# Windowed attention and two MLPs on one core: tiles 6 to 8 turned by VectorE and DRAM, their scores moved into the second chunk

## The chip, the cores and the metric

The kernel runs on one core of one Trainium2 chip. The metric is the device time of a run in microseconds (us); lower is better. Outputs are fp32.

## The reference

```python
scores = (1 / np.sqrt(64)) * np.matmul(q, k.transpose(0, 1, 3, 2))     # 4 x 8 x 576 x 64
rel = pos[:, None] - pos[None, :]
scores = np.where((rel >= 0) & (rel < 64), scores, -1e9)
attn = np.exp(scores - scores.max(-1, keepdims=True))
attn = attn / (attn.sum(-1, keepdims=True) + 1e-9)
x = np.matmul(attn, v).transpose(0, 2, 1, 3).reshape(2304, 512)
...
h = x @ w_in                       # 512 -> 2048, first MLP
x = np.maximum(0.01 * h, h) @ w_out
...
h = x @ w_in2                      # 512 -> 2048, second MLP
out = (np.maximum(h, 0) + np.log1p(np.exp(-np.abs(h)))) @ w_out2
```

## The kernel before, in words

The 2304 tokens are 18 tiles of 128 tokens. Three tiles make a chunk of 384 tokens, so there are six chunks. A tile goes through attention: scores of a 64-wide window on TensorE (`tile_bp`, tile names `ps`), mask and maximum on VectorE (`att_bm` L503, `att_bn` L509), exponentials on ScalarE (`att_be` L520), one over the sums on VectorE (`att_bs`), the product with it on GpSimd (`att_bx` L533), probabilities turned so that keys lie on partitions (into `pair`), and probabilities times values on TensorE (`tile_dp` L909, name `po`). A chunk then goes through the first MLP: for each of 16 steps j a block of 12 matmuls makes 128 hidden columns (`gemm1_p`, name `ph`), ScalarE applies the activation (`gemm1_a` L630, name `g`) and rounds it (`gemm1_h`, `gh`), VectorE takes the rest (`gemm1_l` L642, `gl`), and a second block of 12 matmuls adds it to the output (`gemm2`, name `o`). Every fp32 product is made of three products of rounded high and low parts (`three`, L610 to L612).

The first chunk's steps 0 to 7, then the whole second chunk, are written out by hand in the string `HEAD`, one token for each piece of work, and `ordered` ties each engine's instructions to that order. Tokens are a letter and a number. `G`, `P`, `Q`, `R`, `H` are the five pieces of an MLP step (`gemm1_p`, `gemm1_a`, `gemm1_h`, `gemm1_l`, `gemm2`); numbers 0 to 7 are the first chunk's steps, 8 to 23 the second chunk's, so `P17` makes the tile `g_1_9`. `l`, `a`, `b`, `c`, `d` load one 512 KB weight piece (`wraw`, from `load_w` L147 or L152, three buffers) and convert it: `a` on ScalarE (L161), `b` on VectorE (L166, L168), `c` the high part, `d` the low part on VectorE (L246). `l18`/`l19` are step 9's pieces `wraw_9_0`/`wraw_9_1`, `l20` is `wraw_10_0`, `l24` is `wraw_12_0`. `Lq`, `Lv` load queries and keys, and values; `Bx`, `Cp`, `Ca`, `Dp` are pieces of attention by group (two groups to a tile: 10 and 11 are tile 5), `Cp` is four TensorE transposes (`att_cp` L542, name `pt`) and `Ca` ScalarE's copy of them into `pair`.

After `HEAD` a loop runs the first chunk's steps 8 to 15, then chunks 2 to 5. It has two slots for each step; the table `SLOTS` says in which slot each tile of the next chunk begins its scores and in which its `po` comes, and `attention_slots` hangs the other pieces on these. Tiles 6 to 8 (chunk 2) are prepared in the first chunk's steps 8 to 15, tiles from 9 on during chunks 2 to 5.

From tile `BY_DVE` = 6 on, queries and keys are not transposed by TensorE. `lay_out` (L405) re-lays them through DRAM, from `q`, `k` into `qd`, `kd`, by DMAs of 128-byte runs that SP issues; each is called a relay below. `load_blocks` (L414) brings a tile's part back, and VectorE transposes 32x32 blocks (`tile_u` L889, L890). From tile 9 on the probabilities go a like way: `turn` (L924) transposes blocks on VectorE into `pair`, `cross` writes `pair` to DRAM, `back` reads it in four DMAs. Tiles 6 to 8 have their probabilities turned by TensorE (`att_cp`) and copied by ScalarE (`att_ca`).

The relays of the second and third batch element (`relay`) are not tied to the order: the scheduler puts them among the weight loads on SP, the one engine that issues these DMAs.

Of the kernel before, what the change touches and what calls it, by code (L numbers as in the profile page):

```python
# [8 lines left out]
F32 = mybir.dt.float32  # L9
# [12 lines left out]
def tile_window_attention_two_mlps(  # L22
# [387 lines left out]
    def load_blocks(t):  # L410
        for n, (src, nm) in enumerate(((qd, "q"), (kd, "k"))):
            a = kept[("part", "cv")[n]][:, 2 * DM :] if t >= THIRDS else kept["64"][t % 2].bitcast(F32)[:, n * DM : (n + 1) * DM]
            a = a.rearrange("p (n x) -> p n x", n=NP)
            nc.sync.dma_start(a, src[:, :, t * P : (t + 1) * P])  # L414
            qk_raw[nm, t] = a
# [501 lines left out]
    in_blocks = lambda h: pair[:, h].rearrange("r p x -> r (p x)").rearrange("r (a p c) -> r p a c", p=NP, c=TB)  # L917

    def turn(g):


        t, h = g
        sm = st.pop(g)
        nc.vector.transpose(in_blocks(h), sm.rearrange("r p (b c) -> r p b c", c=TB))  # L924
        st[g] = in_blocks(h)

    def cross(t):

# [14 lines left out]
    def attention_slots(c, n_slots):  # L943

        at = {}
        late = n_slots > 16
        put = lambda n, *todo: at.setdefault(n if late else max(n, -3), []).extend(todo)
        for n in range(TPC):
            t = c * TPC + n
            s, d = SLOTS.get(c, LATER)[n]  # L950
            two = ((t, 0), (t, 1))
            put(s - 6, (att_ah, (t,)))
            put(s - 3, (tile_u, (t,)))
            put(s - 2, (att_aq, (t, "")))
# [17 lines left out]
    SLOTS = {2: ((0, 6), (5, 11), (10, 15)), 3: ((1, 12), (10, 21), (19, 30))}  # L972
# [24 lines left out]
        d14 G7 Be10 a11 Q5 d13 P6 Bs10 Q6 a16 R6 Bx11 Bx10 P7 Cp10 b11 Lv5 b16 Cp11 l15 Ca11 H6 Ca10 c11  # L997
        Dp5 a18 d11 Q7 R5 c16 H5 Dh5 l17 a15 b18 Dl5 G8 d16 b15 c18v a17 P8 c15v R7 d15 G16 P16 G11 P11
# [5 lines left out]
        R18 P9 P21 d23 G22 Q9 R9 H9 c31v Q21 R21 d31 G23 H20 P22 Q19 P23 H21 H18 Q23 R19 Q22 H19 R23 R22  # L1004
# [44 lines left out]
    relay = {CUT + NF - AHEAD - 2 + n: (lay_out, first, range(n * PARTS // 2, (n + 1) * PARTS // 2)) for n in range(2)}  # L1049
    relay |= {CUT + NF - AHEAD + n: (lay_out, first + 1, range(n * PARTS // 4, (n + 1) * PARTS // 4)) for n in range(4)}  # L1050
    begun = 0

    for item in HEAD:
        name = item.rstrip("vg")
        kind = name.rstrip("0123456789")
        n = int(name[len(kind) :])

        held.pop(next((ps for ps, f in READ.items() if f == kind), "") + f"_{n}", None)
        if kind == "G":
            if not begun:  # L1060
                att_tags[:] = ["att"]
            if begun in relay:
                f, *a = relay[begun]
                f(*a)
            if begun == CUT + NF - AHEAD:
                keep_places()
                load_qk(BY_DVE)
                load_qk(BY_DVE + 1)
                load_v(BY_DVE)
            begun += 1  # L1070
        if kind in pieces_by:
            ordered(queues, pieces_by[kind], n, item[len(name) :])
        else:
            ordered(queues, pieces[kind], n)

# [25 lines left out]
    at_slot = {}  # L1101
    base = {}
    slot = 0
    for n, (c, j, s, e, nxt) in enumerate(steps):
        if n < CUT + NF:
            continue
        if s and nxt is not None:
            left = next(i for i in range(n, len(steps)) if steps[i][3]) - n + 1
            base[c] = 2 * (n - CUT - NF), 2 * left, nxt
    for first_slot, n_slots, nxt in base.values():  # L1110
        for i, todo in attention_slots(nxt, n_slots).items():
            at_slot.setdefault(first_slot + i, []).extend(todo)
    for i in sorted(at_slot):
        if i < 0:
            for f, a in at_slot[i]:
                ordered(queues, f, *a)

    for n, (c, j, s, e, nxt) in enumerate(steps):
# [6 lines left out]
        strict = True  # L1125
        run = (lambda f, *a: ordered(queues, f, *a)) if strict else (lambda f, *a: f(*a))
        for u in range(2):
            todo = at_slot.get(2 * (n - CUT - NF) + u, ())
            on_pe = (tile_bp, att_cp)
            run(save_x2)  # L1130
            for f, a in todo:
                if f in on_pe:
                    run(f, *a)
                elif f is tile_d:
                    run(tile_dp, a[0], ((a[0], 0), (a[0], 1)))
            if u == 0:
                run(gemm1_p, c, j)
            elif strict:
                run(gemm1_a, c, j)
                run(gemm1_h, c, j)  # L1140
            for f, a in todo:
                if f is tile_d:
                    x = x_of(a[0] // TPC)
                    run(att_dh, a[0], "", x[0])
                    run(att_dl, a[0], *x)
                elif f not in on_pe:
                    run(f, *a)
            if u == 1 and strict:
                run(gemm1_l, c, j)
            for _ in range(ticks(c, j, u)):  # L1150
                if strict:
                    run(next, keeper, None)
                else:
                    later(next, keeper, None, lag=1)
# [139 lines left out]
```

## Time and profile before

| what | value |
|---|---|
| runs | 838.16, 838.77, 841.83 us; median 838.77 |
| the profiled run's own time | 839.48 us |
| its span, first to last instruction | 837.7 us |
| TensorE busy | 819.9 us, 98% of the span |
| VectorE, ScalarE, GpSimd busy | 616.2, 431.8, 209.0 us |
| DMA | 157.99 MB, mean 189 GB/s |
| granted TensorE clock, mean over the span | 1.000 of full speed |

The profiled run's own time is its span and what lies around it, 1.8 us here. The profile's chain is the work that ended last, followed back from the last instruction: what lies on it sets the time.

### The profile page before, as it was taken

How to read it: one execution, taken by the hardware profiler on the slowest of the kernel's cores; microseconds unless marked ns; L12 is line 12 of the kernel's file. 1: busy time of each engine (PE TensorE's matmuls, PEld its weight loads, DVE VectorE, ACT ScalarE, POOL GpSimd, SP SyncE). 2: the span in 40 equal slices, each digit the busy share in tenths (PEclk: the TensorE clock that was granted, in tenths of full speed). 3: DMA queues.
4: the chain of work that ended last, by engine and by line, in shares of the span. 5: the costliest groups of instructions: out<-in, count | busy, mean ns of one | idle time of the engine just before them, and what ended most of it. 6: DMA issues, size and time to landing. Idle time of an engine off the chain costs nothing.

```text
span 837.7 us, 16547 instructions
## 1 busy us (share of the span) xinstructions
PE 819.9 (98%) x6096; PEld 803.4 (96%) x6096; DVE 616.2 (74%) x1152; ACT 431.8 (52%) x981; POOL 209.0 (25%) x262
## 2 busy tenths in 40 slices
PE   5899999999999999999999999999999999999997
PEld 4799999999999999999999999999999999999997
DVE  5987763446555655554458799998889998989896
ACT  6966533544444454444466655656544454445342
POOL 3211000213333332233125415555511700000000
PEclk9999999999999999999999999999999999999999
DMA  9977667646998979978595544535568884343423
GB/s 224 245 208 201 179 160 140 173 91 188 229 243 253 261 194 253 274 215 219 184 262 170 183 152 148 177 128 169 178 211 264 258 301 151 101 152 101 139 66 100
DMA packets 225505, 157.99 MB, mean 189 GB/s; under 512 B 105488, under 2 KB 194704, under 8 KB 225424
## 3 DMA queue, kind: packets, MB, share of 16 engines
q1 hardware_dynamic: 225424, 156.93, 65.6%
q8 instruction: 48, 0.79, 0.4%
q14 instruction: 33, 0.27, 0.1%
HBM read 103.94 MB, written 59.24 MB: 195 GB/s over the span
## 4 chain that ended last, share of the span: by engine, by line
PE 95%; DVE 2%; DMA 1%; ACT 1%; issue 1%; POOL 0%; SPq 0%; DVEq 0%; ACTq 0%; POOLq 0%
PE ph L610 8%; PE o L610 8%; PE ph L611 8%; PE ph L612 8%; PE o L612 8%; PE o L611 8%; PE f L854 7%; PE f L846 7%; PE f L853 7%; PE p L612 7%; PE p L611 7%; PE p L610 7%; PE po L909 2%; PE ps L485 2%; PE pt L542 1%
## 5 line engine op out<-in xcount | busy, mean ns | idle before, releaser
L610 PE MATMUL ph<-xh,w 128*128 128x384 f32 x384 | 130.5, 340 | 0.0
L610 PE MATMUL o<-gh,w 128*128 128x384 f32 x384 | 130.1, 339 | 0.0
L612 PE MATMUL ph<-xh,w 128*128 128x384 f32 x384 | 128.6, 335 | 0.0
L611 PE MATMUL ph<-xl,w 128*128 128x384 f32 x384 | 128.6, 335 | 0.0
L611 PE MATMUL o<-gl,w 128*128 128x384 f32 x384 | 128.5, 335 | 0.0
L642 DVE TENSOR_TENSOR gl<-g,gh 128x384 fp32r<-128x384 f32 x96 | 57.2, 595 | 90.6 <-ACT gh L636 88.9
L630 ACT ACTIVATE g<-ph 128x384 f32<-128x384 f32 x96 | 46.7, 489 | 145.6 <-PE ph L612 138.2
L612 PE MATMUL o<-gh,w 128*128 128x384 f32 x360 | 120.5, 335 | 0.0
L533 POOL TENSOR_TENSOR sm<-sm,sums 128x512 f32<-128x512 f32 x36 | 39.4, 1095 | 146.4 <-DVE sums L529 135.5
L610 PEld LDWEIGHTS ph<-xh,w 128*128 128x128 f32 x384 | 72.1, 188 | 1.9 <-issue 1.2
L610 PEld LDWEIGHTS o<-gh,w 128*128 128x128 f32 x384 | 72.1, 188 | 1.6 <-issue 1.0
L611 PEld LDWEIGHTS ph<-xl,w 128*128 128x128 f32 x384 | 72.2, 188 | 0.2 <-DVE xl L560 0.2
L612 PEld LDWEIGHTS ph<-xh,w 128*128 128x128 f32 x384 | 72.1, 188 | 0.2 <-DVE w L246 0.2
L611 PEld LDWEIGHTS o<-gl,w 128*128 128x128 f32 x384 | 72.1, 188 | 0.0
L854 PE MATMUL f<-wq,a 128*128 128x256 f32 x252 | 71.5, 284 | 0.0
L853 PE MATMUL f<-wq,a 128*128 128x256 f32 x252 | 71.4, 283 | 0.0
L846 PE MATMUL f<-wq,a 128*128 128x256 f32 x252 | 71.4, 283 | 0.0
L612 PEld LDWEIGHTS o<-gh,w 128*128 128x128 f32 x360 | 67.6, 188 | 0.0
L520 ACT ACTIVATE sm<-sm,nm 128x128 f32<-128x128 f32 x144 | 55.9, 392 | 7.5 <-DVE nm L509 7.5
L636 ACT CAST gh<-g 128x384 fp32r<-128x384 f32 x96 | 49.2, 513 | 15.2 <-PE o L612 11.5
L854 PEld LDWEIGHTS f<-wq,a 128*128 128x128 f32 x252 | 48.4, 192 | 0.2 <-DVE a L803 0.2
L853 PEld LDWEIGHTS f<-wq,a 128*128 128x128 f32 x252 | 48.4, 192 | 0.0
(310 smaller groups left out, 2185.5 us busy)
## 6 DMA issues: line engine op xcount, KB each, us to landing
in<-hd SPq DMA_DIRECT2D x32, 512.0 KB, 4.8
wraw<-in_moe_w_in_dram SPq DMA_DIRECT2D x16, 512.0 KB, 4.0
wraw<-in_moe_w_out_dram SPq DMA_DIRECT2D x16, 512.0 KB, 4.4
kept<-in_moe_w_in_dram SPq DMA_DIRECT2D x16, 512.0 KB, 5.8
kept<-in_moe_w_out_dram SPq DMA_DIRECT2D x16, 512.0 KB, 4.4
hd<-kept SPq DMA_DIRECT2D x19, 384.0 KB, 2.6
hd<-cv SPq DMA_DIRECT2D x15, 384.0 KB, 2.6
wd<-cv SPq DMA_DIRECT2D x11, 512.0 KB, 5.9
```

The source lines that it names most:

```text
L485: nc.tensor.matmul(ps[h][o, p, :], qT[r, p, o], kT[t][r, p, w0 : w0 + P], start=True, stop=True,)
L520: nc.scalar.activation(sm[:, p, :], sm[:, p, :], AF.Exp, bias=nm[:, p : p + 1], accum_out=sums[:, p : p + 1],)
L533: nc.gpsimd.tensor_tensor(sm, sm, sums.unsqueeze(2).to_broadcast([P, NP, P]), ALU.mult)
L610: nc.tensor.matmul(ps, wh, xh, start=start, stop=False)
L611: nc.tensor.matmul(ps, wh, xl, start=False, stop=False)
L612: nc.tensor.matmul(ps, wl, xh, start=False, stop=stop)
L630: nc.scalar.activation(g, ph, AF.Prelu, alpha=0.01)
L636: a = nc.scalar.copy(gh, g)
L642: b = nc.vector.tensor_tensor(gl, g, gh.bitcast(F32), ALU.subtract)
L846: j = nc.tensor.matmul(ps, gh, wh, start=first and u == 0, stop=False, skip_group_check=True)
L853: nc.tensor.matmul(ps, gh, wl, start=False, stop=False, skip_group_check=True)
L854: j = nc.tensor.matmul(ps, gl, wh, start=False, stop=end, skip_group_check=True)
```

## The change

1. Tiles 6 to 8 now use `turn`, `cross` and `back`. Six groups of four TensorE transposes and six ScalarE copies go; six VectorE block transposes of 128x512, three DMAs of 512 KB and twelve of 128 KB come. Tile 7 uses the buffer `cv` where the others use `pair`.
2. `SLOTS[2]` moves the three tiles earlier. Tile 6's scores now come inside `HEAD`, ahead of `G19`, tile 7's ahead of `H9`, tile 8's in slot 3 of the loop. For that the slots are planned ahead (`plan`, `slots_until`, `rest`).
3. The relays are now tied to the order: four at each of eight `G` tokens for the second batch element, four at each of eight for the third.
4. Tiles 6 and 7 load their blocks into the buffers `raw` and `sm` instead of `kept`.
5. Three places of `HEAD` are reordered: `Cp11` is now ahead of `Bx10` and `Cp10` where `Cp11` was, `R5` is ahead of `d11`, `R19` ahead of `H18`.

```diff
     def load_blocks(t):
         for n, (src, nm) in enumerate(((qd, "q"), (kd, "k"))):
-            a = kept[("part", "cv")[n]][:, 2 * DM :] if t >= THIRDS else kept["64"][t % 2].bitcast(F32)[:, n * DM : (n + 1) * DM]
+            if t < BY_DVE + 2:
+                tag, bufs = (("raw", 2), ("sm", 3))[n]
+                a = sb.tile([P, NP, P], F32, tag=tag, bufs=bufs, name=f"{nm}blocks_{t}")
...
+    pair_of = lambda t: cv_pair if t == BY_DVE + 1 else pair
...
     def attention_slots(c):
...
-            put(s - 3, (tile_u, (t,)))
-            put(s - 2, (att_aq, (t, "")))
+            put(s - 3 - (t == BY_DVE + 1), (tile_u, (t,)))
+            put(s - 2 - (t == BY_DVE + 1), (att_aq, (t, "")))
...
-            if late:
-                put(s + 3, *((turn, (g,)) for g in two), (cross, (t,)))
-                put(s + 7, (back, (t,)))
-            else:
-                put(s + 4, *((att_cp, (g,)) for g in two), *((att_ca, (g,)) for g in two))
+            put(s + 3, *((turn, (g,)) for g in two), (cross, (t,)))
+            put(s + 7, (back, (t,)))
...
-    SLOTS = {2: ((0, 6), (5, 11), (10, 15)), 3: ((1, 12), (10, 21), (19, 30))}
+    SLOTS = {2: ((-12, 0), (-3, 8), (3, 15)), 3: ((1, 12), (10, 21), (19, 30))}
...
-        d14 G7 Be10 a11 Q5 d13 P6 Bs10 Q6 a16 R6 Bx11 Bx10 P7 Cp10 b11 Lv5 b16 Cp11 l15 Ca11 H6 Ca10 c11
-        Dp5 a18 d11 Q7 R5 c16 H5 Dh5 l17 a15 b18 Dl5 G8 d16 b15 c18v a17 P8 c15v R7 d15 G16 P16 G11 P11
+        d14 G7 Be10 a11 Q5 d13 P6 Bs10 Q6 a16 R6 Bx11 Cp11 Bx10 P7 b11 Lv5 b16 Cp10 l15 Ca11 H6 Ca10 c11
+        Dp5 a18 R5 d11 Q7 c16 H5 Dh5 l17 a15 b18 Dl5 G8 d16 b15 c18v a17 P8 c15v R7 d15 G16 P16 G11 P11
...
-    relay = {CUT + NF - AHEAD - 2 + n: (lay_out, first, range(n * PARTS // 2, (n + 1) * PARTS // 2)) for n in range(2)}
-    relay |= {CUT + NF - AHEAD + n: (lay_out, first + 1, range(n * PARTS // 4, (n + 1) * PARTS // 4)) for n in range(4)}
+    relay = {5 + n: (lay_out, first, range(n * PARTS // 8, (n + 1) * PARTS // 8)) for n in range(8)}
+    relay |= {14 + n: (lay_out, first + 1, range(n * PARTS // 8, (n + 1) * PARTS // 8)) for n in range(8)}
...
             if begun in relay:
                 f, *a = relay[begun]
-                f(*a)
+                ordered(queues, f, *a)
```

Three places show what moves. The first is SP, the queue that issues the DMAs, from the load of step 9's first weight piece on. Before:

```order
L147 DMA wraw_9_0_959<-in_moe_w_in_dram 128x4x128
L372 DMA vs_1019<-in_v_dram 128x8x64
L372 DMA vn_1021<-in_v_dram 128x8x64
L405 DMA qd<-in_q_dram 32x12x32
L152 DMA wraw_7_1_1030<-in_moe_w_out_dram 128x512
L152 DMA wraw_8_1_1086<-in_moe_w_out_dram 128x512
L405 DMA kd<-in_k_dram 32x12x32
L405 DMA qd<-in_q_dram 32x12x32
L152 DMA wraw_9_1_1147<-in_moe_w_out_dram 128x512
```

and now:

```order
L147 DMA wraw_9_0_967<-in_moe_w_in_dram 128x4x128
L405 DMA qd<-in_q_dram 32x12x32
L405 DMA kd<-in_k_dram 32x12x32
...
L372 DMA vs_1031<-in_v_dram 128x8x64
L372 DMA vn_1033<-in_v_dram 128x8x64
L152 DMA wraw_7_1_1042<-in_moe_w_out_dram 128x512
L152 DMA wraw_8_1_1098<-in_moe_w_out_dram 128x512
...
L152 DMA wraw_9_1_1171<-in_moe_w_out_dram 128x512
L152 DMA wraw_10_1_1178<-in_moe_w_out_dram 128x512
L147 DMA wraw_10_0_1181<-in_moe_w_in_dram 128x4x128
```

Four relays now stand ahead of tile 5's values (`vs`, `vn`), and at the second line of dots there are twelve relays between `wraw_8_1` and `wraw_9_1`, where there were two. Behind `wraw_10_0` come eight relays, then `wraw_11_0` and `wraw_13_0`, four relays, `wraw_14_0`, four relays, the two block loads of tile 6, and `wraw_12_0`.

The second place is TensorE at the end of `HEAD`, between the last `o` block of the second chunk and the third `ph` block after it. Before, the two groups of tile 6 are transposed there:

```order
L612 MATMUL o_0_3_1240<-gh_15_1753,w_last 128x384
L542 MATMUL pt_0_1905<-ident,sm_0_1814 128x128 x4
L542 MATMUL pt_1_1910<-ident,sm_1_1816 128x128 x4
L610 MATMUL ph_10_1915<-xh_0_496,w_1180 128x384
L611 MATMUL ph_10_1915<-xl_0_497,w_1180 128x384
```

These two rows are gone, and so are the like pairs of tiles 7 and 8. Tile 6's scores now stand in the second chunk, ahead of the block `G19`:

```order
L616 MATMUL o_0_3_1272<-gh_2_1458,w_200 128x384
L489 MATMUL ps_0_1511<-kT_1345,qbd 64x128 x2
L489 MATMUL ps_1_1512<-kT_1345,qbd 64x128 x2
...
L614 MATMUL ph_11_1529<-xh_1_748,w_1291 128x384
L615 MATMUL ph_11_1529<-xl_1_749,w_1291 128x384
```

The scores are as many as before; they have only moved.

The third is VectorE after `H11`, where tile 6's turn now stands among the weight conversions (the cast and the L246 row of `w_1659` are `c30` and `d30`; `sums` are tile 6's):

```order
L246 TENSOR_TENSOR w_1502<-cv,w_1502 128x512
L532 TENSOR_SCALAR sums_0_1592<-sums_0_1592 128x4
L533 RECIPROCAL sums_0_1592<-sums_0_1592 128x4
...
L930 STREAM_TRANSPOSE pair<-sm_0_1550 128x4x4x32
L930 STREAM_TRANSPOSE pair<-sm_1_1552 128x4x4x32
L466 CAST w_1659<-cv 128x512
L246 TENSOR_TENSOR w_1659<-cv,w_1659 128x512
L166 TENSOR_SCALAR cv<-cv 128x512
L168 SCALAR_TENSOR_TENSOR cv<-wraw_11_1_1581,cv 128x512
```

Before, the cast of `w_1570` followed the first of these rows at once. On ScalarE the token `a31` stands behind `d30`, and `P19` (the tile `g_1_11`) behind `a31`.

## Rows read from the trace of the kernel before

**Rows 1.** The page: span, DMA rate in 40 slices, and the chain by engine.
```profile
span 837.7 us, 16547 instructions
...
GB/s 224 245 208 201 179 160 140 173 91 188 229 243 253 261 194 253 274 215 219 184 262 170 183 152 148 177 128 169 178 211 264 258 301 151 101 152 101 139 66 100
...
PE 95%; DVE 2%; DMA 1%; ACT 1%; issue 1%; POOL 0%; SPq 0%; DVEq 0%; ACTq 0%; POOLq 0%
```

**Rows 2.** PE's timeline (start, duration, instructions [idle <-releaser]): tile 5's transposes and `po`.
```profile
68.44 1.10 PE L542 MATMUL pt<-ident,sm 128*128 128x128 f32 x8 [0.91 <-POOL sm L533]
...
71.58 0.69 PE L909 MATMUL po<-pair,vs 128*64 128x64 f32 x16
```

**Rows 3.** PE's timeline, end of `HEAD`: tile 6's scores and transposes, tile 7's scores.
```profile
139.94 1.10 PE L485 MATMUL ps<-kT,qbd 64*64 64x128 f32 x32 [0.45 <-ACT qbd L469]
...
149.43 1.03 PE L542 MATMUL pt<-ident,sm 128*128 128x128 f32 x8
...
152.48 1.10 PE L485 MATMUL ps<-kT,qbd 64*64 64x128 f32 x32
```

**Rows 4.** PE's timeline: tile 4's queries and keys are transposed (`Ap4`).
```profile
27.80 0.63 PE L458 MATMUL pq<-ident,qraw 128*128 128x128 f32 x4 [0.81 <-DMA qraw<-in_q_dram]
29.10 0.63 PE L458 MATMUL pk<-ident,kraw 128*128 128x128 f32 x4 [0.67 <-DMA kraw<-in_k_dram]
```

**Rows 5.** PE's timeline, first matmul of the blocks `G14` and `G15`.
```profile
87.33 0.33 PE L610 MATMUL ph<-xh,w 128*128 128x384 f32 x1
...
99.81 0.33 PE L610 MATMUL ph<-xh,w 128*128 128x384 f32 x1
```

**Rows 6.** SP's timeline of DMA issues: the first relay.
```profile
16.52 0.88 SPq L405 DMA_DIRECT2D qd<-in_q_dram  x1
```

**Rows 7.** SP's timeline: first and last of twelve relays issued one behind another.
```profile
114.51 0.62 SPq L405 DMA_DIRECT2D qd<-in_q_dram  x1
...
121.88 0.63 SPq L405 DMA_DIRECT2D kd<-in_k_dram  x1
```

**Rows 8.** SP's timeline: tile 5's `vs`, a relay, `wraw` 7_1/8_1, 13_0, 14_0/12_0.
```profile
64.20 0.51 SPq L372 DMA_DIRECT2D vs<-in_v_dram  x1
...
65.64 1.88 SPq L405 DMA_DIRECT2D qd<-in_q_dram  x1
70.21 1.44 SPq L152 DMA_DIRECT2D wraw<-in_moe_w_out_dram  x2
...
87.63 0.37 SPq L147 DMA_DIRECT2D wraw<-in_moe_w_in_dram  x1
...
90.03 4.49 SPq L147 DMA_DIRECT2D wraw<-in_moe_w_in_dram  x2
```

**Rows 9.** DMA issues: KB of each, median us from issue to landing.
```profile
wraw<-in_moe_w_in_dram SPq DMA_DIRECT2D x16, 512.0 KB, 4.0
...
vs<-in_v_dram SPq DMA_DIRECT2D x16, 256.0 KB, 5.2
```

**Rows 10.** ACT's timeline: `a20` and `P17`; `a24`, then `P13` and `P12`.
```profile
84.64 0.67 ACT L161 ACTIVATE cv<-wraw 128x512 f32<-128x512 f32 x1
...
85.95 0.51 ACT L630 ACTIVATE g<-ph 128x384 f32<-128x384 f32 x1
...
97.99 0.66 ACT L161 ACTIVATE cv<-wraw 128x512 f32<-128x512 f32 x1 [2.16 <-DMA wraw<-in_moe_w_in_dram]
98.55 0.85 ACT L630 ACTIVATE g<-ph 128x384 f32<-128x384 f32 x2
```

**Rows 11.** Windows: us, PE busy, PEld, DVE, ACT, POOL busy (instructions), clock, DMA share, GB/s.
```profile
100.00:110.00 10.00, 10.00 (x59) 10.00 (x59) 8.07 (x15) 5.23 (x11) 0.00 (x0) 1.00 0.76 183
110.00:120.00 10.00, 10.00 (x60) 10.00 (x59) 7.65 (x16) 4.26 (x10) 0.00 (x0) 1.00 0.63 155
```

**Rows 12.** Lines of DVE, `turn`: xcount | busy us, mean ns | idle before.
```profile
L924 DVE STREAM_TRANSPOSE pair<-sm 128x512 f32<-128x512 f32 x18 | 12.1, 695 | 3.3 <-POOL sm L533 3.1
```

**Rows 13.** POOL's timeline: the second product of tile 6.
```profile
148.14 1.04 POOL L533 TENSOR_TENSOR sm<-sm,sums 128x512 f32<-128x512 f32 x1 [0.41 <-ACT g L630]
```

More of the change, by code (lines that the diff above doesn't have):

```diff
@@ L411, in load_blocks @@
         for n, (src, nm) in enumerate(((qd, "q"), (kd, "k"))):
-            a = kept[("part", "cv")[n]][:, 2 * DM :] if t >= THIRDS else kept["64"][t % 2].bitcast(F32)[:, n * DM : (n + 1) * DM]
-            a = a.rearrange("p (n x) -> p n x", n=NP)
+            if t < BY_DVE + 2:
+                tag, bufs = (("raw", 2), ("sm", 3))[n]
+                a = sb.tile([P, NP, P], F32, tag=tag, bufs=bufs, name=f"{nm}blocks_{t}")
+            else:
+                a = kept[("part", "cv")[n]][:, 2 * DM :] if t >= THIRDS else kept["64"][t % 2].bitcast(F32)[:, n * DM : (n + 1) * DM]
+                a = a.rearrange("p (n x) -> p n x", n=NP)
             nc.sync.dma_start(a, src[:, :, t * P : (t + 1) * P])
@@ L941, in tile_d, with attention_slots @@
         pass
-    def attention_slots(c, n_slots):
+    def attention_slots(c):
         at = {}
-        late = n_slots > 16
-        put = lambda n, *todo: at.setdefault(n if late else max(n, -3), []).extend(todo)
+        put = lambda n, *todo: at.setdefault(n, []).extend(todo)
         for n in range(TPC):
@@ L1048, in tile_window_attention_two_mlps, with plan, slot_before, slot_after @@
     first = BY_DVE * P // S
-    relay = {CUT + NF - AHEAD - 2 + n: (lay_out, first, range(n * PARTS // 2, (n + 1) * PARTS // 2)) for n in range(2)}
-    relay |= {CUT + NF - AHEAD + n: (lay_out, first + 1, range(n * PARTS // 4, (n + 1) * PARTS // 4)) for n in range(4)}
+    relay = {5 + n: (lay_out, first, range(n * PARTS // 8, (n + 1) * PARTS // 8)) for n in range(8)}
+    relay |= {14 + n: (lay_out, first + 1, range(n * PARTS // 8, (n + 1) * PARTS // 8)) for n in range(8)}
+    at_slot = {}
+    def plan():
+        for n, (c, j, s, e, nxt) in enumerate(steps):
+            if s and nxt is not None:
+                for i, todo in attention_slots(nxt).items():
+                    at_slot.setdefault(2 * (n - CUT - NF) + i, []).extend(todo)
+    def slot_before(todo, run):
+        for f, a in todo:
+            if f is tile_bp:
+                run(f, *a)
+            elif f is tile_d:
+                run(tile_dp, a[0], ((a[0], 0), (a[0], 1)))
+    def slot_after(todo, run):
+        for f, a in todo:
+            if f is tile_d:
+                x = x_of(a[0] // TPC)
+                run(att_dh, a[0], "", x[0])
+                run(att_dl, a[0], *x)
+            elif f is not tile_bp:
+                run(f, *a)
+    waiting = []
+    def rest():
+        while waiting:
+            slot_after(waiting.pop(0), lambda f, *a: ordered(queues, f, *a))
+    def slots_until(n):
+        rest()
+        for i in sorted(i for i in at_slot if i <= n):
+            rest()
+            todo = at_slot.pop(i)
+            slot_before(todo, lambda f, *a: ordered(queues, f, *a))
+            waiting.append(todo)
+    plan()
     begun = 0
@@ L1074, in tile_window_attention_two_mlps @@
             ordered(queues, pieces[kind], n)
+        if kind == "P":
+            rest()
     def later(f, *a, lag=LAG2):
@@ L1099, in finish @@
             put_x2(c)
[L1101 to L1116, printed above, removed]
+    slots_until(-1)
+    rest()
     for n, (c, j, s, e, nxt) in enumerate(steps):
@@ L1124, in tile_window_attention_two_mlps @@
             keep_last()
-        strict = True
-        run = (lambda f, *a: ordered(queues, f, *a)) if strict else (lambda f, *a: f(*a))
+        run = lambda f, *a: ordered(queues, f, *a)
         for u in range(2):
             todo = at_slot.get(2 * (n - CUT - NF) + u, ())
-            on_pe = (tile_bp, att_cp)
             run(save_x2)
[L1131 to L1135, printed above, removed]
+            slot_before(todo, run)
             if u == 0:
                 run(gemm1_p, c, j)
-            elif strict:
+            else:
                 run(gemm1_a, c, j)
                 run(gemm1_h, c, j)
[L1141 to L1148, printed above, removed]
+            slot_after(todo, run)
+            if u == 1:
                 run(gemm1_l, c, j)
             for _ in range(ticks(c, j, u)):
[L1151 to L1154, printed above, removed]
+                run(next, keeper, None)
         if c == 0 and j >= NF - 4:
```

30 lines of the change are left out of this document (17 added, 13 removed).

## The prediction

> **What bounds the kernel now.** I read the page first. TensorE holds 95% of the chain that ended last [rows 1], so a change moves the time by what it takes off TensorE's own work, or by the waits that it makes or removes in front of TensorE. Nearly all the remaining question is therefore local: who arrives late at which block. I then read TensorE's timeline for gaps. From 35 us to the end of the hand-written order there are only two worth naming: 0.91 us ahead of tile 5's transposes, on GpSimd's product [rows 2], and 0.45 us ahead of tile 6's scores, on ScalarE [rows 3]. Before 35 us TensorE waits for tile 4's queries and keys, 0.81 and 0.67 us [rows 4]. Last I read SP's and ScalarE's timelines, since the change moves 12 of 32 relays to one place in front of weight loads; what counts is how much slack those loads have at the blocks `G14` and `G15`.
>
> A measurement of this kernel can tell about 0.5%, 4.2 us, from no change. The profiled run's own time, 839.48, lies 0.71 us above the median of the runs; differences are worked out in the profiled execution and set against the median 838.77.
>
> **What goes.** (a) The transposes of tiles 6 to 8. From tile 6's eight transposes to the next scores it is 3.05 us [rows 3], and between lies one block of 12 matmuls. From `G14` to `G15` six such blocks take 12.48 us, 2.08 each [rows 5]. One tile's transposes so cost 0.97 us of TensorE, three cost **2.9 us**, all on the chain. ScalarE loses six copies; it has room there, so I count nothing for them.
>
> (b) The 0.45 us ahead of tile 6's scores goes with those scores, which now stand in the second chunk: **-0.45**. Late there next would be tile 7's scores, dealt with under (g).
>
> (c) `Cp11` ahead of `Bx10`: half of the eight transposes can run while TensorE waits for `Bx10` [rows 2]. Their half is worth 0.4 us, and the wait of 0.91 is long enough to take it. It counts only until the next wait swallows it, see (e).
>
> (d) Two relays leave the start, at 16.52 [rows 6]. In a row a relay goes out every 0.67 us (twelve from 114.51 to 121.88, [rows 7]), so two are 1.3 us of the queue ahead of tile 4's keys. The waits at `Ap4` sum to 1.48 [rows 4]. Bounds: no gain, if those loads are held by something else, and 1.3. I take **-0.6**, between.
>
> **What comes.** (e) Tile 5's values. They were issued at 64.20 [rows 8]; four relays now stand ahead, 4 x 0.67 = 2.7, so 66.9. With 5.2 us to landing [rows 9] they are there at 72.1; tile 5's `po` began at 71.58 [rows 2] and would now begin 0.4 earlier. TensorE waits about 0.9. Bounds: none, if the load lands sooner in an emptier queue, and 2.5, if the relays go out as slowly as the one that took 1.88 [rows 8].
>
> (f) The weights. `wraw_7_1` and `wraw_8_1` wait for buffers until 71.65 [rows 8]. Then come twelve relays, 8.0 us, so that `wraw_9_1`, `wraw_10_1`, `wraw_10_0` go out at 79.7, 80.1 and 80.5. The fullest slice of the span moves 301 GB/s [rows 1], 1.74 us for 512 KB; the first lands 4.0 after issue [rows 9], the third by that pace 3.5 later, at 87.2. ScalarE works in order: `a20` needs the third, and from its start to the end of `P17` it is 1.8 us (84.64 to 86.46, [rows 10]). `G14` takes the accumulator that `P17` empties; it started at 87.33 [rows 5]. Now `P17` ends at 89.0 to 89.5: `G14` is 2.3 us later than before. Bounds: 0.7, if the three land with no queueing, 3.0, if the relays still in flight slow them. The 0.5 left over from (c) and (e) lies inside this 2.3, it is not added.
>
> The next is `wraw_12_0`, for `a24`, which already waits 2.16 us for its data [rows 10]. `wraw_13_0` waited for a buffer until 87.63 [rows 8]; 2.3 later that is 89.9. Behind it come four relays, `wraw_14_0`, four more and two block loads, ten issues of 0.67: `wraw_12_0` goes at about 97.4, against 94.1 before (90.03 and 4.49 less its own issue, [rows 8]). It lands at 101.4 to 102.4. From `a24`'s start to the end of `P13` it is 1.0 us, and `G15` (99.81, [rows 5]) needs that end: 102.5 to 103.4. `G15` is then 3.4 us later than before, bounds 2.0 and 4.5, the upper if the block loads of 512 KB in front cost their 1.74 too. So loads and waits up to here together are **+3.4**, measured against the old time of `G15`.
>
> A relay is 32x12x32 numbers, 48 KB, in 0.67 us: 73 GB/s, against 301 in the fullest slice. The Trainium skill, "DMA: Bandwidth & Descriptors", section Specifications, says that a transfer needs at least 512 bytes to go at line rate; these runs are 128 bytes. It speaks against a bunch of relays ahead of loads, and by it I would take the upper bounds in (f), +4.5 for +3.4; no row here shows a bunch of relays right ahead of loads, so the trace does not decide it.
>
> (g) VectorE. Tile 6's two transposes of queries and keys, its mask and maximum and its turn, and tile 7's two transposes now lie between about 100 and 130 us, where VectorE also converts weights. From 100 to 120 it is busy 15.7 of 20 us [rows 11]. Six transposes of 0.695 [rows 12] make 19.9. Both turns wait for GpSimd, and `d30`, `a31` and `P19` stand behind them, on which `G21` depends. In the trace GpSimd ended with tile 6 9.2 us after its scores began (139.94 to 149.18, [rows 3, 13]). Two turns are 1.4 more, `d30`'s two operations about 1.2, `a31` and `P19` about 1.2 [rows 10], 13.0 in all. `G21` is due 13.5 us after the scores begin, their 1.04 and six blocks. So it just holds, if nothing else stands in between. I take **+0.4**, bounds 0 and 1.5. The twelve `back` and three `cross` DMAs lie behind the weights and have a slot distance of four and more; I cost them at nothing; their cover is the four slots between turn and use, and if it is gone `po` of tile 7 is late first.
>
> **Sum.** -0.6 (d) + 3.4 (c, e, f) - 0.45 (b) - 2.9 (a) + 0.4 (g) = -0.15 us: **838.6 us**. With the low ends, -1.3 + 2.0 - 0.45 - 2.9, it is 836.1; with the high ends, 4.5 - 0.45 - 2.9 + 1.5, it is 841.4.
>
> **Rivals.**
>
> *The loads are hidden.* If the weights keep their slack at `G14` and `G15`, only gains are left: 0.6 + 0.4 + 0.45 + 2.9 = 4.35, **834.4 us**. For it: ScalarE is busy only 5.23 and 4.26 of 10 us a little later [rows 11], so it could catch up, and a relay may cost less where the queue is empty. Against: `a24` already waits for its data by 2.16 us, and twelve relays come in one piece. Chance 0.15.
>
> *The relays go slowly.* The place is the twelve relays ahead of `wraw_9_1`. There 0.67 us each was taken from a stretch (110 to 120) in which the DMA engines were 0.63 busy [rows 11]; a single relay among weight loads took 1.88 us [rows 8]. Each 0.1 us on the twelve is 1.2 us at `G14`. At the middle, 1.28, `G14` is 7.3 us later still: **845.9 us**. From 1.04 us a relay on, the kernel is slower by over 0.5%. Against it: with twelve in a row the last goes out as quickly as the first, 0.63 and 0.62 [rows 7]. Chance 0.12.
>
> *VectorE is the bound.* If the four mask and maximum operations, each as long as a turn, also fall between 100 and 120, VectorE has 22.7 us of work in 20, and `G21` is 2.7 late instead of 0.4: **840.9 us**. For it: the chain through GpSimd. Against: 13.0 of 13.5 us leaves a little room, and part of this work falls behind 120. The Trainium skill, "VectorE: DVE Perf Modes", section Rules for kernel authors, says to transpose 128x128 on TensorE where PSUM will do as the place; that is the advice which this change goes against. By that rule the time would be this rival's; the trace, with TensorE on the chain and 0.97 us a tile there, does not bear it out so far. Chance 0.13.
>
> **How the numbers follow.** My forecast has 0.60. Faster by over 0.5% (below 834.6) is a little over half of the first rival, 0.09; slower by over 0.5% (above 843.0) is the slow relays, 0.12; the rest, 0.79, is within. The range leaves out the slow relays and the lower half of the first rival, 834.3 to 843.0; my forecast's own is 836.1 to 841.4.
>
> **What would show it.** After the change: no rows of transposes (L546) behind 75 us; a wait of TensorE on the values load near 72; `G14` and `G15` 2 to 4 us later than 87.33 and 99.81, with ScalarE's `a20` and `a24` waiting for DMA; no wait ahead of tile 6's scores; from `HEAD`'s end on, the distance to the old times shrinking by about 1 us at each tile. If `G15` keeps its old time, (f) is wrong; if `G21` waits by more than 2 us, the third rival holds; if `wraw_9_1` goes out after 84 us, the second.

## The result and the profile after

The changed kernel takes 846.56 us, median of 6 runs (844.96 to 849.94), against 838.56 for the kernel before (838.16 to 841.83): the ratio is 1.0087, 95% interval 1.0059 to 1.0115. That is 8.0 us slower, 0.9%, for which I had a chance of 0.12, and outside the predicted range, 834.3 to 843.0. The profiled run took 846.16, its span is 844.3.

The page of the changed kernel, to be held against [rows 1]:

```profile
span 844.3 us, 16526 instructions
...
PE 821.6 (97%) x6072; PEld 804.3 (95%) x6072; DVE 621.0 (74%) x1158; ACT 428.7 (51%) x975; POOL 209.8 (25%) x262
...
PE 88%; ACT 3%; DVE 3%; DMA 2%; SPq 2%; issue 1%; POOL 0%; DVEq 0%; ACTq 0%; POOLq 0%
```

The 24 transposes are gone (6072 instructions of TensorE for 6096), and still TensorE holds 88% of the chain where it held 95%. ScalarE, VectorE, DMA and SP's queue hold 10% of it where they held 4%. TensorE is even busy for 1.7 us longer with less work. Both need an explanation; the first is in its waits. The waits of TensorE in the changed kernel (engine, what it waited for: us in total, times, longest us):

```profile
PE ph L614 <- ACT g L634: 6.4, 2, 3.5
...
PE o L615 <- DVE gl L646: 0.4, 1, 0.4
```

The first row is new: two waits for ScalarE's activation, 6.4 us. TensorE's timeline of the changed kernel (start, duration, instructions, [idle before <-releaser]) shows where they are:

```profile
66.81 1.03 PE L546 MATMUL pt<-ident,sm 128*128 128x128 f32 x8
...
89.47 0.44 PE L614 MATMUL ph<-xh,w 128*128 128x384 f32 x1 [3.55 <-ACT g L634]
...
91.23 0.52 PE L616 MATMUL ph<-xh,w 128*128 128x384 f32 x1
...
99.51 0.33 PE L614 MATMUL o<-gh,w 128*128 128x384 f32 x1
...
106.64 0.44 PE L614 MATMUL ph<-xh,w 128*128 128x384 f32 x1 [2.80 <-ACT g L634]
...
114.58 0.33 PE L614 MATMUL o<-gh,w 128*128 128x384 f32 x1
...
149.19 0.45 PE L615 MATMUL o<-gl,w 128*128 128x384 f32 x1 [0.40 <-DVE gl L646]
```

The first row answers to [rows 2]: tile 5's transposes start 1.63 us earlier, with no wait. The second and the fifth are `G14` and `G15`, which stood at 87.33 and 99.81 [rows 5]. So `G14` is 2.14 late, as predicted (2.3), and `G15` 6.83, twice what was predicted (3.4). Between them lies something that no wait shows. From `G14` to `H17` (99.51) are four blocks, 4 x 2.08 = 8.32 us; they took 10.04, 1.72 too long. From `G15` to `H13` (114.58) are three, 6.24 us; they took 7.94, 1.70 too long. The windows of 1 us say why (stretch: length, PE busy, PEld, DVE, ACT, POOL busy, then the granted clock, DMA share, GB/s):

```profile
86.00:87.00 1.00, 0.00 (x0) 0.00 (x0) 0.18 (x1) 1.00 (x3) 0.00 (x0) 1.00 0.36 63
...
90.00:91.00 1.00, 1.00 (x7) 1.00 (x6) 1.00 (x3) 0.00 (x0) 0.00 (x0) 0.85 0.92 302
91.00:92.00 1.00, 1.00 (x5) 1.00 (x4) 0.97 (x3) 0.00 (x0) 0.00 (x0) 0.50 0.53 144
...
94.00:95.00 1.00, 1.00 (x6) 1.00 (x6) 0.69 (x1) 0.12 (x1) 0.00 (x0) 0.94 0.92 169
...
108.00:109.00 1.00, 1.00 (x5) 1.00 (x4) 0.92 (x2) 0.46 (x2) 0.00 (x0) 0.50 1.08 333
```

Behind each wait the granted clock falls to 0.50, that is from 2.4 to 1.2 GHz, for about 3.4 us, and a matmul takes 0.52 us there (the row at 91.23) for 0.33 at full clock (the row at 99.51). These 1.72 and 1.70 us are the longer busy time with less work.

ScalarE's timeline shows what the waits are made of:

```profile
82.84 0.66 ACT L161 ACTIVATE cv<-wraw 128x512 f32<-128x512 f32 x1 [2.23 <-DMA wraw<-in_moe_w_out_dram]
85.62 0.66 ACT L161 ACTIVATE cv<-wraw 128x512 f32<-128x512 f32 x1 [2.13 <-DMA wraw<-in_moe_w_out_dram]
...
87.62 0.66 ACT L161 ACTIVATE cv<-wraw 128x512 f32<-128x512 f32 x1
...
88.91 0.51 ACT L634 ACTIVATE g<-ph 128x384 f32<-128x384 f32 x1
...
105.55 0.66 ACT L161 ACTIVATE cv<-wraw 128x512 f32<-128x512 f32 x1 [5.86 <-DMA wraw<-in_moe_w_in_dram]
106.11 0.86 ACT L634 ACTIVATE g<-ph 128x384 f32<-128x384 f32 x2
```

The first four rows are `a19`, `a21`, `a20` and `P17`, the last two `a24` and `P13`, `P12`; `a20`, `P17` and the last two answer to [rows 10]. Two weights come late, `wraw_9_1` and `wraw_10_1`, and ScalarE waits for each in order; the third, `wraw_10_0` for `a20`, is there when its turn comes. The activation that empties `G14`'s accumulator stands behind all three; the same again, with one weight, at `G15`. And SP's queue shows why the weights are late:

```profile
65.32 0.56 SPq L372 DMA_DIRECT2D vs<-in_v_dram  x1
...
68.63 1.45 SPq L152 DMA_DIRECT2D wraw<-in_moe_w_out_dram  x2
70.13 0.56 SPq L405 DMA_DIRECT2D qd<-in_q_dram  x1
...
77.95 0.62 SPq L405 DMA_DIRECT2D kd<-in_k_dram  x1
78.68 1.02 SPq L152 DMA_DIRECT2D wraw<-in_moe_w_out_dram  x2
79.80 0.38 SPq L147 DMA_DIRECT2D wraw<-in_moe_w_in_dram  x1
...
100.02 0.55 SPq L147 DMA_DIRECT2D wraw<-in_moe_w_in_dram  x1
```

The twelve relays stand between 70.13 and 78.57, 0.70 us each (predicted 0.67), and `wraw_9_1`, `wraw_10_1`, `wraw_10_0` behind them. The last row is `wraw_12_0`: it goes out at 100.02 (predicted 97.4) and takes 5.5 us until ScalarE has it at 105.55, against a median of 4.0 [rows 9].

### The profile page after: what moved, and what is told of

The parts are those of the page before. It is cut to its first block, busy times and chain, and to the rows that moved or that the text cites. A ratio compares the mean times of both kernels' runs of the same rounds, so it can differ in the third digit from the quotient of the medians.

```text
span 844.3 us, 16526 instructions
## 1 busy us (share of the span) xinstructions
PE 821.6 (97%) x6072; PEld 804.3 (95%) x6072; DVE 621.0 (74%) x1158; ACT 428.7 (51%) x975; POOL 209.8 (25%) x262
## 4 chain that ended last, share of the span: by engine, by line
PE 88%; ACT 3%; DVE 3%; DMA 2%; SPq 2%; issue 1%; POOL 0%; DVEq 0%; ACTq 0%; POOLq 0%
PE ph L614 7%; PE f L858 7%; PE f L850 7%; PE f L857 7%; PE ph L616 7%; PE ph L615 7%; PE o L614 7%; PE p L614 7%; PE p L616 7%; PE p L615 7%; PE o L615 7%; PE o L616 7%; PE po L913 2%; PE ps L489 2%; ACT sm L524 1%; SPq L405 1%
```

## The experiments

Theory A: the relays ahead of weight loads make ScalarE late, TensorE waits for activations that stand behind these weights on ScalarE, and each long wait is paid twice, by itself and by the slow clock behind it. Theory B: the attention pieces in the second chunk cost the time. In every comparison the kernel before ran on the same chip; its medians were 838.4 to 838.6.

**The relays alone**, on the kernel before.

```diff
-    relay = {CUT + NF - AHEAD - 2 + n: (lay_out, first, range(n * PARTS // 2, (n + 1) * PARTS // 2)) for n in range(2)}
-    relay |= {CUT + NF - AHEAD + n: (lay_out, first + 1, range(n * PARTS // 4, (n + 1) * PARTS // 4)) for n in range(4)}
+    relay = {5 + n: (lay_out, first, range(n * PARTS // 8, (n + 1) * PARTS // 8)) for n in range(8)}
+    relay |= {14 + n: (lay_out, first + 1, range(n * PARTS // 8, (n + 1) * PARTS // 8)) for n in range(8)}
...
-                f(*a)
+                ordered(queues, f, *a)
```

> The kernel before with part 3 of the change alone: the relays in their new places on SP, everything else as it was (TensorE still transposes tiles 6 to 8, HEAD and SLOTS as before). Theory A, the relays ahead of the weight loads make the loss: TensorE waits about 3 us at G14 and 2 to 3 us at G15 for ScalarE, which waits for weights, and after each of the two waits the granted clock is 0.5 for about 4 us, 1.7 us lost each. The wait of 0.91 ahead of tile 5's transposes stays, and neither -0.45 nor -2.9 is gained, so some 9 us over the kernel before, 846 to 849 us. Theory B, the loss comes from the attention pieces put into the second chunk: no such waits, 837.5 to 839 us.

844.13 us, ratio 1.0070 (1.0047 to 1.0093). Without any attention piece moved, 5.5 us of the 8 are there, so B is not needed for them. The profiled run is the fastest of the five (842.34 us), so its trace shows only a part of that. TensorE's timeline has the wait at `G14`, and the clock falls behind it (0.50 from 90 to 93 us):

```profile
88.86 0.44 PE L610 MATMUL ph<-xh,w 128*128 128x384 f32 x1 [2.13 <-ACT g L630]
```

I expected a second wait at `G15`; there is none. Tile 6's block loads, which the change puts ahead of `wraw_12_0`, are not there, that load goes out at 97.57 and `a24` starts at 101.79, just in time.

**The relays earlier.**

```diff
-    relay = {5 + n: (lay_out, first, ...
+    relay = {n: (lay_out, first, ...
-    relay |= {14 + n: (lay_out, first + 1, ...
+    relay |= {16 + n: (lay_out, first + 1, ...
```

> The changed kernel with the second element's relays at the first eight G tokens instead of the sixth to thirteenth, so that none lies between wraw_8_1 and wraw_14_0, and the third element's two steps later, so that none lies ahead of wraw_12_0. Theory A: both waits (3.55 us at G14, 2.80 at G15) and the slow clock behind them (3.4 us together) go, 9.7 us, unless the relays cost something ahead of 50 us; 835 to 838 us. If the relays hold up the loads at 35 to 50 us instead, the waits reappear there and it is 839 to 843. Theory B: 846 us as the changed kernel.

845.56 us, ratio 1.0074 (1.0050 to 1.0099). The waits at `G14` and `G15` are gone, and a longer one stands where the relays now are; ScalarE waited 5.99 us for a weight at 50.94:

```profile
55.85 1.12 PE L913 MATMUL po<-pair,vs 128*64 128x64 f32 x16 [5.88 <-ACT g L634]
```

The wait follows the relays. This is A, in its unfavourable branch, and worse than the 839 to 843 that I gave for it.

**The third element's relays two steps later.**

```diff
-    relay |= {14 + n: (lay_out, first + 1, ...
+    relay |= {16 + n: (lay_out, first + 1, ...
```

> The changed kernel with the third element's relays two steps later alone: eight relays less ahead of wraw_12_0, the twelve ahead of wraw_9_1 stay. Theory A: the wait at G14 stays at 3.55 us with its slow clock; wraw_12_0 goes out some 5 us sooner, so the wait at G15 goes, wholly or all but 0.5 us, and with it the second slow stretch, 4.5 us: 841 to 843 us. If wraw_12_0 is held by something other than the relays ahead of it (its buffer), the wait at G15 stays, 846 us.

842.00 us, ratio 1.0027 (1.0006 to 1.0047), 4.6 us less than the change: the wait at `G15` goes, the one at `G14` stays:

```profile
90.91 0.69 PE L614 MATMUL ph<-xh,w 128*128 128x384 f32 x1 [3.71 <-ACT g L634]
...
106.06 0.33 PE L614 MATMUL ph<-xh,w 128*128 128x384 f32 x1
```

The time is as expected, the reason only in part. The ten runs lie between 838.38 and 844.42, and the profiled one is the slowest of them. In it the second row, `G15`, starts only 0.58 us sooner than in the change (106.64): the wait is gone there in part because TensorE itself comes later from `G14`, and the second slow stretch (1.70 us) goes with it. `wraw_12_0` goes out no sooner (100.38), but `a24` has it 3.7 us later instead of 5.5; what stands ahead of it on SP is the same but for these relays. What holds this load is its buffer, last read by the conversion `b22` on VectorE. The last row of `b22` in the kernel before, in the change and in this run:

```profile
93.32 0.75 DVE L168 SCALAR_TENSOR_TENSOR cv<-wraw,cv 128x512 uint16<-128x512 uint32 x1
...
97.18 0.76 DVE L168 SCALAR_TENSOR_TENSOR cv<-wraw,cv 128x512 uint16<-128x512 uint32 x1
...
99.57 0.75 DVE L168 SCALAR_TENSOR_TENSOR cv<-wraw,cv 128x512 uint16<-128x512 uint32 x1
```

It ends at 94.07, 97.94 and 100.32, and `wraw_12_0` goes out at 94.1, 100.02 and 100.38. So before the change and in this run the load goes as soon as its buffer is free; in the change the queue holds it 2.1 us longer.

**The waits filled.** Matmuls that nothing uses are put into the two waits, so that TensorE is busy in them.

```diff
+    FILL = {14: 18, 15: 15}
+    def fill(step, count):
+        ...
+        for i in range(count):
+            nc.tensor.matmul(spare, wh[:, 0, :], xh[:, 0, :], start=True, stop=True)
...
             slots_until(2 * (begun - CUT - NF))
+            if n in FILL:
+                ordered(queues, fill, steps[n], FILL[n])
```

> The changed kernel with matmuls that nothing uses put ahead of G14 (18 of 128x384) and G15 (15 of 128x384) into a spare accumulator, about 3.1 and 2.6 us of TensorE time inside the waits. Theory A with the clock as a cost of its own: the waits stay as long in the clock of the loads (TensorE is busy, not idle), G14 and G15 begin at the same moment after the loads, but the granted clock stays 1.0 behind them, so that 3.4 us come back: 842 to 844 us. Rival: the clock falls for another reason than the idle stretch, or the 3.4 us were hidden by later waits: 846 to 847 us.

844.32 us, ratio 1.0065 (1.0042 to 1.0087), 2.2 us less than the change by the medians; the runs of the two overlap (842.99 to 846.18 here). In the profiled run the clock stays at full speed but for the last microsecond of the span, and what is left of the two waits and of the stretch behind them is this:

```profile
core 0: 842.6 us, clock 1.000
```

```profile
105.72 0.44 PE L614 MATMUL ph<-xh,w 128*128 128x384 f32 x1 [0.57 <-ACT g L634]
...
118.19 0.44 PE L614 MATMUL ph<-xh,w 128*128 128x384 f32 x1 [0.77 <-ACT g L634]
```

So the slow clock comes from the idle stretch and not from the load of the chip: with TensorE kept busy it does not fall. Its cost is nearer to 2.2 us than to 3.4: the timeline, too, has `H13` only 2.5 us sooner (112.07 for 114.58). The first row says why: `G15` starts only 0.92 us sooner than in the change (106.64), since it waits for `wraw_12_0` in either case. Nearly half of the first slow stretch was hidden in the second wait.

**Relays in the gaps, scores six steps later.** An attempt at a version that keeps the gains.

```diff
-                put(s - 8, (load_qk, (t,)))
+                put(s - 6, (load_qk, (t,)))
...
-    relay = {5 + n: ...
-    relay |= {14 + n: ...
+    relay = {20 + n: (lay_out, first + 1, range(n * PARTS // 4, (n + 1) * PARTS // 4)) for n in range(4)}
+    GAPS = {"l13": 4, "l14": 1, "l11": 2, "l16": 3, "l18": 2, "l17": 1, "l19": 1, "l21": 1, "l20": 3, "l22": 2, "l26": 3, "l25": 3, "l30": 2, "l29": 4}
...
+        if name in GAPS:
+            ordered(queues, lay_out, first, range(laid[0], laid[0] + GAPS[name]))
+            laid[0] += GAPS[name]
...
-    SLOTS = {2: ((-12, 0), (-3, 8), (3, 15)), ...
+    SLOTS = {2: ((-6, 5), (0, 11), (5, 15)), ...
```

> A version made from theory A: the changed kernel, but one to four relays of the second element right behind single weight loads, as the kernel before had them in the gaps, the third element's eight at each of the last four G tokens, and tile 6's scores six steps later (SLOTS of chunk 2: -6 and 5, 0 and 11, 5 and 15), since its blocks need all relays of the second element. Theory A: the waits at G14 and G15 go with their slow clock, the gains stay (2.9 for the transposes, 0.45, and about 1.6 at the start and tile 5): 833.5 to 836 us. Rival, SP or the DMA engines are simply full in this stretch, wherever the relays stand: waits of 1 to 4 us at other weights, and a slow stretch behind each over 2 us, 838 to 844 us.

847.48 us, ratio 1.0088 (1.0066 to 1.0110). No wait at `G14` or `G15`: with one to four relays behind each load the weights are in time. But three others have come, further on:

```profile
128.73 0.44 PE L614 MATMUL o<-gh,w 128*128 128x384 f32 x1 [2.02 <-ACT gh L640]
...
138.90 0.69 PE L615 MATMUL o<-gl,w 128*128 128x384 f32 x1 [3.03 <-DVE gl L646]
...
162.72 1.97 PE L489 MATMUL ps<-kT,qbd 64*64 64x128 f32 x28 [2.87 <-DVE xl L564]
```

At 136.32 VectorE had waited 6.76 us for tile 7's blocks, behind 24 relays of the third element. The attempt is a miss of its own making; what it shows is that these relays, moved from one stretch, hold up what is loaded in the next.

**ScalarE's order, first step.**

```diff
-... G17 G10 F7 a20 E7 R16 P17 b21 ...
+... G17 G10 F7 E7 R16 P17 a20 b21 ...
-... d20 a24 P13 d26 P12 b24 ...
+... d20 P13 d26 P12 a24 b24 ...
```

> The changed kernel with two places of HEAD reordered, relays where the change has them: a20 behind P17, and a24 behind P13 and P12, so that ScalarE no longer makes the activations that empty accumulators wait behind a weight that has not landed. Theory A in its narrow form (the order on ScalarE turns a late weight, needed much later, into a wait of TensorE): the wait at G14 shrinks from 3.55 to under 1 us (a19 and a21, also late, still stand ahead of P17, so 1.5 to 3 are possible) and that at G15 goes; the slow clock goes where a wait falls under 1 us: 838 to 842 us. Rival: the weights are needed as late as they land, so that the waits move to the blocks that read them: 845 to 847 us.

845.35 us, ratio 1.0070 (1.0051 to 1.0089). The wait at `G14` shrinks by 0.43 us only, since `a19` and `a21` still stand ahead of `P17` and each waits over 2 us. The one at `G15` is gone, and its lateness comes out in pieces behind it, through ScalarE's and VectorE's order:

```profile
88.83 0.44 PE L614 MATMUL ph<-xh,w 128*128 128x384 f32 x1 [3.12 <-ACT g L634]
110.20 0.45 PE L615 MATMUL o<-gl,w 128*128 128x384 f32 x1 [0.59 <-DVE gl L646]
113.84 0.44 PE L615 MATMUL o<-gl,w 128*128 128x384 f32 x1 [1.28 <-DVE gl L646]
119.28 0.44 PE L614 MATMUL ph<-xh,w 128*128 128x384 f32 x1 [2.21 <-ACT g L634]
```

The time is the rival's: with the relays where the change has them, some weights are too late for this order. The fuller order below was not run with those relays.

**HEAD's three reorderings alone**, on the kernel before.

> The kernel before with the three reorderings of HEAD alone (part 5). By the prediction's (c): half of the transposes run inside the wait of 0.91 us, 0.4 us less: 838.2 us. By the changed kernel's trace, where that wait is gone altogether: 0.9 less, 837.7 us. Either lies at the edge of what the rounds can tell; the profile tells the two apart by the wait that is left ahead of tile 5's transposes.

838.37 us, ratio 0.9998 (0.9984 to 1.0012). The wait ahead of tile 5's transposes is gone in the profile (they start at 66.64, for 68.44 before), the median does not move. Only 0.91 of these 1.80 us is that wait; the rest is gained earlier, where nothing was changed. The profile shows the mechanism; whether the 0.9 us arrive is not settled.

**ScalarE's order in full**, with the third element's relays two steps later.

```diff
-... l19 b17 d18 Q16 l21 a19 l20 a21 b19 c17 Q8 d17 R8 H7 c19 G17 G10 F7 a20 E7 R16 P17 b21 Q17 G14
+... l19 b17 d18 Q16 l21 l20 c17 Q8 d17 R8 H7 G17 G10 F7 E7 R16 P17 a19 a21 b19 c19 a20 b21 Q17 G14
-... d20 a24 P13 d26 P12 b24 ...
+... d20 P13 d26 P12 a24 b24 ...
-    relay |= {14 + n: ...
+    relay |= {16 + n: ...
```

> The changed kernel with the relays of the third element two steps later, as in the run that did this alone, and ScalarE's order changed further: a19, a21 and a20 all behind P17, with b19 and c19 behind them, and a24 behind P13 and P12. Theory A, narrow form: no activation that empties an accumulator stands behind a late weight, so both waits go and no slow stretch follows: 835 to 838 us. Rival: the weights themselves are late for the blocks that read them (G11 to H17), and TensorE waits there instead, 2 us or more with a slow stretch behind: 841 to 845 us.

837.68 us, ratio 0.9986 (0.9973 to 1.0000): 8.9 us less than the change, with every part of it in place but for the third element's relays, which stand two steps later. Theory B falls with it: the attention pieces stand in the second chunk as in the change. The twelve relays still stand ahead of `wraw_9_1`; what they delay is now needed by nobody at once. TensorE's waits behind 70 us are small, and the clock is at full speed until the last 3 us of the span:

```profile
70.14 0.69 PE L913 MATMUL po<-pair,vs 128*64 128x64 f32 x16 [0.17 <-ACT cv L161]
110.53 0.44 PE L614 MATMUL ph<-xh,w 128*128 128x384 f32 x1 [0.38 <-ACT g L634]
117.56 0.44 PE L615 MATMUL o<-gl,w 128*128 128x384 f32 x1 [0.34 <-DVE gl L646]
140.26 0.44 PE L615 MATMUL o<-gl,w 128*128 128x384 f32 x1 [0.39 <-DVE gl L646]
251.18 0.69 PE L913 MATMUL po<-pair,vs 128*64 128x64 f32 x16 [0.40 <-DVE nm L513]
```

It has the lowest median of all versions, level with the kernel before or 0.8 us below it.

**The turn alone**, on the kernel before: tiles 6 to 8 by `turn`, `cross`, `back` in the loop, SLOTS of chunk 2 at (0, 9), (3, 12), (6, 15), `back` three slots earlier.

> The kernel before with the transposes of tiles 6 to 8 moved to VectorE and DRAM and nothing in HEAD or on SP before its end changed: their scores stay in the loop (slots 0, 3, 6; po in 9, 12, 15; back three slots earlier than in the change, so that it fits). It measures what parts 1 and 2 are worth where the relays stay in the old gaps. If the prediction's (a) holds, TensorE's 24 transposes give 2.9 us and the wait of 0.45 ahead of tile 6's scores stays: 835.5 us, faster by 0.35%. Rival, the way through DRAM is too long here: TensorE waits 1 to 3 us at a po for the four back DMAs, with a slow stretch behind a wait of over 2 us: 837 to 841 us.

845.29 us, ratio 1.0078 (1.0059 to 1.0098). Tile 7's values are late, a fault of this run: SP issued them at 172.13, behind other DMAs, and the clock fell while TensorE waited (0.50 from 173 to 182 us). The first row, tile 5's transposes, stands for later: they start 0.63 us sooner than in the kernel before [rows 2], with the same wait, though nothing ahead of them was changed.

```profile
67.81 1.09 PE L542 MATMUL pt<-ident,sm 128*128 128x128 f32 x8 [0.91 <-POOL sm L533]
...
176.29 1.12 PE L909 MATMUL po<-cv,vs 128*64 128x64 f32 x16 [6.18 <-issue]
```

**The turn alone, values in two parts**, without and with HEAD's reorderings.

```diff
+            if t == BY_DVE:
+                put(s, (load_part, (t + 1, 0)))
+                put(d, (load_part, (t + 1, 1)), (load_part, (t + 2, 0)))
+            elif t == BY_DVE + 1:
+                put(d, (load_part, (t + 1, 1)))
```

> The run with the turn alone failed in its own way: tile 7's values were loaded 4 us before their po, behind other issues of SP. Here half of each tile's values is loaded as soon as a buffer is free, the rest right behind the po that frees it, and back one slot later; else the same: the kernel before with tiles 6 to 8 turned by VectorE and DRAM in the loop, relays and HEAD as before. If (a) holds, 2.9 us off: 835.5 us. Rival: the values or the back DMAs still come late, a wait of 1 to 3 us at a po with a slow stretch behind: 837 to 841 us.

842.01 us, ratio 1.0039 (1.0025 to 1.0053).

> The same with part 5 of the change, the three reorderings of HEAD, which took away the wait ahead of tile 5's transposes in the profile and nothing in the median. If the two add up: 835 to 835.5 us, a version faster than both kernels without any relay moved. Rival: as for the run beside it, 837 to 841 us.

841.78 us, ratio 1.0033 (1.0019 to 1.0047). Both keep one long wait, 2.98 and 3.03 us, for the second part of tile 8's values, which stand behind relays of the last element on SP, and a slow stretch behind it:

```profile
184.75 1.12 PE L914 MATMUL po<-pair,vn 128*64 128x64 f32 x16 [2.98 <-DMA vn<-in_v_dram]
...
180.39 1.12 PE L914 MATMUL po<-pair,vn 128*64 128x64 f32 x16 [3.03 <-DMA vn<-in_v_dram]
```

**These relays later too**, two steps.

```diff
-        if c == 0 and j >= NF - 4:
-            run(lay_out, 3, range(4 * (j + 4 - NF), 4 * (j + 5 - NF)))
+        if c == 0 and j >= NF - 2:
+            run(lay_out, 3, range(8 * (j + 2 - NF), 8 * (j + 3 - NF)))
```

> The run before (turn in the loop, values in two parts, HEAD reordered) with one edit more: the relays of the last element, which stood ahead of the second part of tile 8's values on SP, two steps later, eight at a step. There TensorE waited 3.03 us and the clock was slow behind it, 1.7 us. If the late values were all that was left, 841.8 less 4.7, 837 us, and less still, 835.5, if the 2.9 us of the transposes then show in full. Rival: po of tile 8 then waits for the back DMAs instead, 839 to 841 us.

837.95 us, ratio 0.9993 (0.9982 to 1.0003). The long wait goes with its slow stretch, 3.8 us by the medians. What is left of the 2.9 us is 0.4, against HEAD's reorderings alone (838.37), and no more than the spread. The profiled run is the slowest of the twelve, with a wait of 2.66 us for tile 4's keys, ahead of all that this edit moves. Its waits of TensorE in the loop, of which the first two are new:

```profile
PE po L914 <- DMA pair<-turned: 0.9, 1, 0.9
PE ps L490 <- POOL sm L538: 0.6, 1, 0.6
PE ps L490 <- ACT qbd L474: 0.4, 1, 0.4
```

## Why the prediction was wrong, point by point

- **(a), the transposes, -2.9**: over-sized in what arrives. From tile 5's transposes to tile 9's scores TensorE is busy for 116.65 us in the kernel before, 114.78 in the run with ScalarE's order in full and 114.36 in the last run: 1.9 and 2.3 us less. In the change it is 118.20, which less the 3.42 of the slow clock is 114.78 again. Where the rest of the 2.9 goes the runs do not show. Against the gain stand 1.1 us of new waits between 110 and 141 us in the first of these runs, in the last one, with the turn in the loop, 1.5.
- **(b), -0.45**: right, no wait is left ahead of tile 6's scores.
- **(c) and (d), the early gains**: (c) is mis-sized, to the safe side: the wait of 0.91 went wholly in the change's profile. (d) is not shown. Tile 5's transposes start 1.63 us earlier, where I counted 1.0, but beyond that wait this is 0.72, and the run with the turn alone, which moves no relay there, has 0.63 of it.
- **(e), tile 5's values**: no wait, the lowest of the bounds. They went out at 65.32 and not 66.9, because SP was 1.6 us ahead by then; in the filled run, which is otherwise the same there, 0.28 and 0.20 us are seen.
- **(f), the weights, up to `G14`**: late weights on ScalarE were the right mechanism, and `G14` came out almost to the point (2.14 late, predicted 2.3), in part by luck: the twelve relays began 1.5 us sooner than I had them, and it was not the third load that `a20` waited for but the second that held `a21`, 6.2 us from its issue.
- **(f), from `G14` to `G15`**: this is the step that failed: "`wraw_12_0` goes at about 97.4 ... It lands at 101.4 to 102.4". It went out at 100.02 and was there at 105.5; `G15` came 6.83 us late for a predicted 3.4. I took the 94.1 of the kernel before for a place in the queue; it was the buffer, which the late `G14` and the slow clock now free only at 97.94. The queue took 2.1 us more: `wraw_13_0` got its buffer only at 90.5 (I had 89.9), and of the eight relays ahead one took 1.84 us at 92.96 and one 1.00 at 97.47. And the load took 5.5 us for 4.0; the DMA share in 100 to 120 was 0.91 and 0.98, where it had been 0.76 and 0.63 [rows 11]. A size was off, too: the eight relays ahead of this load are the third element's, 72 KB each on the change's page, and so were eight of the twelve in [rows 7], not 48. The Trainium skill, "DMA: Bandwidth & Descriptors", section Specifications, asks for at least 512 bytes for line rate. By that rule I would have taken the upper bounds in (f). The trace agrees with that direction, and goes beyond it: in the filled kernel, without a slow clock, `G15` is still 5.9 us late (105.72), above the +4.5.
- **The clock**, not in the sum at all. The prediction counts a wait by its length alone. Each of the two waits was followed by 3.4 us at half clock, 1.7 us more; filled, they gave back 2.2 us together. This term alone would have put the forecast at 840.8, inside the range still.
- **(g), VectorE, +0.4**: right in size (0.40 at 149.19), in another place than `G21`.
- The sum at tile 9's scores: from tile 5's transposes to there the change takes 124.95 us for 117.10. That is 6.75 of waits (3.55, 2.80, 0.40) less the old 0.45, 3.42 of slow clock, and 1.87 less for the transposes. Less the 1.63 gained ahead it is 6.2 late there, and 6.6 at the end of the span.
- **The rivals**: *the relays go slowly* gave 845.9 and came nearest, but by another way: the twelve went at 0.70 us, not 1.28. It was the loads behind them that slowed, and the clock. *VectorE is the bound* did not decide anything. For the rule cited there (the Trainium skill, "VectorE: DVE Perf Modes", section Rules for kernel authors: TensorE for 128x128 where PSUM will do) the runs speak more than I did: with everything else repaired, the way over VectorE and DRAM is worth 0.4 us in the last run, not to be told from nothing, of some 2 that TensorE saves.

## What to carry to other kernels

An engine that works in order turns any late input into a wait for all that stands behind it: look not at when a late weight is needed but at what is queued behind its first use, and move that ahead; here two lines of order gave back 4.3 us (842.0 to 837.7), with twelve relays still ahead of the weights. Price a DMA that is moved by what lands behind it, and a TensorE wait by the slow clock that may follow it as well, 1.7 us behind each of the two here. Before you price a load by its place in the queue, look whether its buffer is free. And where a saving needs a transfer to be earlier, ask first whether the queue has room there: each place tried here for the relays held up another load.

## What the runs showed of the hardware that I had not expected

The granted clock of a TensorE that is 97% busy over the span falls after a single wait. In the changed kernel it went to 0.50 behind idle stretches of 3.55 and 2.80 us, and was back at 1.00 some 4.5 us after the work resumed. In the profiled runs above it fell as well behind waits of 2.13, 2.46, 2.66, 2.87, 2.98, 3.03 (twice), 3.12, 3.71, 5.88 and 6.18 us. Behind one of 2.02 (relays in the gaps) and one of 2.21 (ScalarE's order, first step) it did not; so the length of a single wait alone does not decide it. Two profiled runs (`HEAD`'s reorderings alone, and the first with values in two parts) also show 0.50 at about 18 to 20 us, behind waits of at most 1.1 us each, one after another. With matmuls that nobody uses in the two waits it did not fall in the profiled run.
